# State space layer and feed-forward on one core: the last stage of the kernel tables is placed behind a pair of first weights on VectorE and handed over four steps later

## The chip, the cores and the metric

The kernel runs on one core of a Trainium2 chip. The core has TensorE (PE; PEld is its weight load), VectorE (DVE), ScalarE (ACT), GpSimd (POOL) and SyncE (SP). Here SP, POOL and ACT also start DMA transfers, each through its own queue. The metric is the device time of one execution in microseconds; the profile shows one such execution, instruction by instruction.

## The reference

The input is normalized, and the output is the input plus two branches computed from the normalized tokens `xn` (2048 tokens of 576 channels): a state space layer, applied as a long convolution through Fourier transforms, and a feed-forward block with 4608 hidden units.

```python
def _A_ref(u, A_re, A_im, B_re, B_im, C_re, C_im, log_dt, Dskip):
    dt = jnp.exp(log_dt)[:, None]
    logdA = dt * (A_re + 1j * A_im)
    dB = dt * (B_re + 1j * B_im)
    P = jnp.exp(logdA[:, :, None] * l[None, None, :])
    K = jnp.einsum("dn,dnl,dn->dl", C_re + 1j * C_im, P, dB).real
    ...
def _B_ref(x, w1, w2):
    h = _silu(jnp.einsum("bsd,df->bsf", x, w1))
    return jnp.einsum("bsf,fd->bsd", h, w2)
xn = _layernorm(x, axis=-1)
return x + _A_ref(xn, ...) + _B_ref(xn, B_w1, B_w2)
```

The factor of each of the 576 x 128 states, C·B·dt, is a complex number. The kernel needs it as a magnitude (the table `rhoT`) and a phase in turns (`phiT`). The stage that this change moves is the last part of that phase: it puts the arctangent into the right octant, and the signs with it.

## The kernel before

**Feed-forward on the path of TensorE.** Every float32 operand is split into a high and a low part, and a product is three matmuls (high·high, high·low, low·high). `ffn` goes over two halves of the tokens, over chunks of four tiles of hidden units, and over two blocks of 512 tokens in a half. `up` (line 312 on) makes one hidden tile: 14 matmuls of 512 columns (L320 to L322) into a PSUM tile `ph`, SiLU on ScalarE (`gf`, L328), a copy as the high part `gh` (ScalarE, L329) and the low part `gl` (VectorE, L330). `down` makes an output tile `po` from four hidden tiles: two groups of 12 matmuls of 288 columns (L350), each added to `acc` on VectorE (L355).

**Weights.** `load_w1` brings two tiles of first weights into `w1r`, of which this stretch has a single buffer, with three DMAs on SP's queue (L266 to L268). `split_w1` makes of them the high parts `w1h` (ScalarE, L288) and the low parts `w1l` (VectorE, L290), and remembers the latest low part as `pins["w1l"]`. The next load into the buffer can start once the second low part has been made. Second weights go likewise through `w2r` (SP, L297), a high part (ScalarE, L306) and a low part (VectorE, L308).

**Work beside it.** `side` is a second generator. In it, `phase0` normalizes the later tokens and turns them on TensorE (L125, L130); ScalarE and VectorE take high and low parts out of PSUM (L126, L128, L131, L132; the tile is `xt`), and POOL's queue stores `xt` to DRAM as `dxt` (L241). `natural` makes the tables in stages that are separated by `yield`; the last one is L772 to L782 on VectorE, eleven operations on 96 x 768, with transposes of `br` and `t0` (L689) and copies into `rhoT` and `phiT` (L690). Behind `natural` comes `kgen`, which makes the convolution kernel in 36 chunks: `magic`, `pw` (L806, L808), angles `th` (L838, L840), a rounding pair (ScalarE L854, VectorE L855), absolute value, sine and cosine on ScalarE (L856 to L858), magnitudes `C` and products `S`, `C` on VectorE (L859 to L875). The tiles of `kgen` lie in memory that `phase0` and `natural` have used, so the first of them, `magic`, can be written only when the last store of `xt` has read its tile.

**What sets the order.** `weave` hands the two generators' instructions over in turns: `ffn` has 276 steps, and `side` goes on when its next mark times 276 is reached. A scheduler then orders each engine's instructions, by this order of handing over and by its own idea of when each is ready. `behind(ins)` adds one constraint: what is traced in it stands behind `ins` on that instruction's engine. Each engine, and each DMA queue, takes its instructions in the order so found.

Of the kernel before, what the change touches and what calls it, by code (L numbers as in the profile page):

```python
# [13 lines left out]
ALU = mybir.AluOpType  # L14
# [27 lines left out]
def kernel(  # L42
# [94 lines left out]
    pins = {}  # L137
    wino = {}

    def behind(ins):  # L140
        return tc.issue_after(ins) if ins is not None else nullcontext()

    def spread(up):

        s1 = up.tile([P, 2, P], F32R, name="s1", bufs=1)
        nc.gpsimd.dma_start(s1, cs1)
        for j in range(NJ):
            src = up.tile([P, D], F32, tag="xr", name="xr")
            nc.sync.dma_start(src, dxn[:, j])
            for m in range(2):  # L150
                lo, hi = slice(64 * m, 64 * m + 64), slice(64 - 64 * m, 128 - 64 * m)
                u1 = up.tile([P, D], F32, tag="u1", name="u1")
                sp = up.tile([P, D], F32R, tag="sp", name="sp")
                nc.scalar.copy(sp[lo, :], src[lo, :])
                nc.vector.tensor_sub(sp[hi, :], src[lo, :], sp[lo, :])
                for h in range(2):
                    hs = slice(h * HD, (h + 1) * HD)
                    pu = pss.tile([P, 512], F32, tag="pss", name="pu")
                    nc.tensor.matmul(pu[:, :HD], s1[:, 0, :], sp[:, hs], start=True, stop=False)  # L159
                    nc.tensor.matmul(pu[:, :HD], s1[:, 1, :], sp[:, hs], start=False, stop=True)  # L160
                    nc.scalar.copy(u1[:, hs], pu[:, :HD])  # L161
                nc.gpsimd.dma_start(  # L162
                    d1u.rearrange("(p m j) d -> m j p d", m=2, j=NJ)[m, j], u1)
                yield j
# [46 lines left out]
    def phase0(p0, js):  # L211
        j0 = js[0]
        if j0 < 8:
            xs = load_x(j0, accp, "acc", (nc.sync,))
            acc.update(zip(js, xs))
            yield
        else:
            xs = load_x(j0, p0, "xj", (nc.sync,))
        if j0:
            with behind(pins["xt1"] if j0 == 2 else None):  # L220
                turned(p0, js, norm(p0, js, xs))
        else:
            xn = [norm(p0, (j,), (xj,)) for j, xj in zip(js, xs)]
            last = pins["xn"]
            for j in js:
                turned(p0, (j,), xn[j], None if j else last)
                pins[f"xt{j}s"] = pins["xt_s"]
# [441 lines left out]
    def natural(nat):  # L669
# [3 lines left out]
        v = nc.vector  # L673

        def tl(name):
            return nat.tile([NP, NT, NS], F32, tag=name, name=name)

        def load(ap, name):
            t = tl(name)
            nc.sync.dma_start(t, ap.rearrange("(p t) n -> p t n", t=NT))  # L680
            return t
# [14 lines left out]
        cr, ci = load(c_re, "cr"), load(c_im, "ci")  # L696
# [63 lines left out]
        rc = tl("are")  # L760
# [8 lines left out]
        with behind(last):  # L769
            nc.scalar.mul(t0, t0, 1.0 / (2 * math.pi))  # L770
        yield
        v.tensor_tensor(rc, ci, cr, op=ALU.is_gt)  # L772
        v.tensor_scalar(t1, t0, -2.0, 0.25, op0=ALU.mult, op1=ALU.add)
        v.tensor_mul(t1, t1, rc)
        v.tensor_add(t0, t0, t1)
# [215 lines left out]
    def tail():  # L991

        def last(j):
            y = yp.tile([P, 2, D], F32, tag="yt", name="yt", bufs=2)
            py = [[pool.tile([P, 512], F32, tag=tag, name="py") for pool, tag in pools]
                  for pools in (((ps2, "ps2"), (pss, "pss")), ((pss, "pss"),) * 2)]
            conv((j, j + 1), py)
            for i in range(2):
                for h in range(2):
                    nc.scalar.copy(y[:, i, h * HD:(h + 1) * HD], py[i][h][:, :HD])  # L1000
                conv_load(j + i + AHEAD)
            store(y, j, (nc.gpsimd,), accum_op=ALU.add)

        steps = [(tail_at[0] + j * tail_at[1], conv_load, j) for j in range(AHEAD)]
        steps += [(tail_at[2] + j * tail_at[3], last, j) for j in range(0, 8, 2)]
        for at, f, j in sorted(steps, key=lambda v: v[0]):
            yield at
            with behind(pins["load"]):
                f(j)
# [45 lines left out]
    def gate_of(i):  # L1055

        return (FT + i * 2 * FT + 1) / (2 * NCH * 2 * 2 * FT)

    def side():
        nonlocal s4, kl, yp, pa, kfp, w1x, tail_at  # L1060
        marks = (0.1357, 0.613, 0.855)
        tail_at = (0.893, 0.003, 0.932, 0.005)
        with tc.tile_pool(name="pa", bufs=4) as pa:
            for js in ((0, 1), (2, 3), (4, 5), (6, 7)):
                with behind(pins["xt3"] if js[0] > 2 else None):
                    for _ in phase0(pa, js):
                        if js[0] <= 2:
                            yield 0
                pins[f"xt{js[1]}"], pins[f"xt{js[1]}s"] = pins["xt_v"], pins["xt_s"]
                if js[0] == 2:  # L1070
                    yield 0
            yield 0
        with tc.tile_pool(name="kf", bufs=1) as kfp:
            for n in ("f", "rho", "phi"):
                kf[n] = kfp.tile([P, D], F32, name=n + "T")
            with tc.tile_pool(name="nat", bufs=1) as nat, tc.tile_pool(name="pb", bufs=2) as pb:
                nt = natural(nat)
                tiles = iter(range(8, NJ, 2))
                for at, tables in ((0.0, 1), (0.02, 0), (0.035, 0), (gate_of(1), 1), (0.06, 0), (gate_of(2), 1), (0.08, 0), (0.085, 1)):
                    yield at  # L1080
                    if tables:
                        next(nt, None)
                    else:
                        j = next(tiles)
                        with behind(pins["gl"]):
                            for _ in phase0(pb, (j, j + 1)):
                                pass
            with behind(pins["sd"]):
                nc.gpsimd.dma_start(f1, cf1)
            nc.sync.dma_start(vt, cv)  # L1090
            with tc.tile_pool(name="up", bufs=1) as up, tc.tile_pool(name="w1x", bufs=1) as more:
                sp = spread(up)
                for n, at in enumerate(kgen()):
                    if n > 1:
                        w1x = more
                        next(sp, None)
                    yield marks[0] + at * (marks[1] - marks[0])
                for _ in sp:
                    pass
        w1x = None  # L1100
        s4p = ctx.enter_context(tc.tile_pool(name="s4p", bufs=1))
        s4 = s4p.tile([P, 32], F32, name="s4")
        nc.gpsimd.dma_start(s4, cs4)

        w1x = ctx.enter_context(tc.tile_pool(name="w1y", bufs=1))
        xp = ctx.enter_context(tc.tile_pool(name="xp", bufs=1))
        with tc.tile_pool(name="sx", bufs=1) as sx, tc.tile_pool(name="sy", bufs=1) as sy:
            for k, _ in enumerate(wino_x(sx, sy, xp)):
                yield (171 + k) / 276
        with tc.tile_pool(name="kl", bufs=1) as kl:  # L1110
            for at in spectral():
                yield 176 / 276 + (at - 1) * (marks[2] - 176 / 276)
        yp = ctx.enter_context(tc.tile_pool(name="yp", bufs=3))
        yield from tail()

    sd, fg = side(), ffn()
    for g in (sd, fg, sd, fg, sd, fg, sd):
        next(g)
# [83 lines left out]
```

## Time and profile before

| | |
|---|---|
| median of 3 runs | 1108.33 us (1106.89 to 1108.94) |
| profiled execution | 1107.62 us |
| its span, first to last instruction | 1105.8 us |
| granted TensorE clock | 1.000 |
| instructions in the span | 23079 |

The span lies 1.8 us inside the time of its execution. Times in the views below count from the span's start. A row of the timeline has the start, the duration, engine, line, operation, output <- inputs, shape and count, and in brackets the idle time ahead of it with what ended it. A row of the waits has who waited, for whom, and the total, count and longest in us.

### The profile page before, as it was taken

To read this page: it belongs to the slowest core of one execution; us is meant where nothing else is said; L and a number is where in the kernel's file an instruction comes from. 1 tells how busy PE (TensorE), PEld (TensorE's weight loads), DVE (VectorE), ACT (ScalarE), POOL (GpSimd) and SP (SyncE) were. 2 spreads that over 40 slices of the span, in tenths; PEclk is the share of its full clock that TensorE was granted. 3 is DMA by queue.
4 is the path that set the end of the run, shared out by engine and by line. 5 is a ranking of instruction groups with operands and counts; after the bars stand their busy time and mean duration, and the time that the engine had idled before them with its cause. 6 is when DMAs were issued, how large, how long until landed. Compare 5 with 4: busy or idle time off the path is not lost.

```text
span 1105.8 us, 23079 instructions
## 1 busy us (share of the span) xinstructions
PE 1088.1 (98%) x9101; PEld 985.9 (89%) x9101; DVE 951.8 (86%) x1615; ACT 722.2 (65%) x1283; POOL 143.3 (13%) x249
## 2 busy tenths in 40 slices
PE   6999999999999999999999999999999999999998
PEld 6989899898998888898999989999999999999787
DVE  7699889999999999999999997988888888886323
ACT  4476457677777676767766746888778878775320
POOL 3212100000000000000220001111111221110220
PEclk9999999999999999999999999999999999999999
DMA  9436552355263535457963236465556565554984
GB/s 289 129 128 202 166 165 94 115 148 155 86 170 110 136 131 128 157 116 255 245 208 74 90 82 196 133 183 173 152 162 176 182 176 176 148 161 114 240 220 110
DMA packets 162908, 173.67 MB, mean 157 GB/s; under 512 B 88416, under 2 KB 128624, under 8 KB 162160
## 3 DMA queue, kind: packets, MB, share of 16 engines
q1 hardware_dynamic: 137312, 105.31, 34.3%
q0 software_dynamic: 24320, 65.38, 19.2%
q10 hardware_dynamic: 1168, 1.51, 0.5%
q8 instruction: 72, 1.18, 0.5%
q14 instruction: 36, 0.29, 0.1%
HBM read 109.64 MB, written 62.60 MB: 156 GB/s over the span
## 4 chain that ended last, share of the span: by engine, by line
PE 84%; DVE 7%; DMA 3%; ACT 3%; issue 1%; SPq 1%; POOL 0%; ACTq 0%; POOLq 0%
PE po L350 36%; PE ph L320 17%; PE pb L477 7%; PE pc L477 3%; PE kp L897 3%; PE pk L1031 2%; PE pu L1031 2%; PE pb L1031 2%; PE pa L477 2%; PE z L912 1%; PE ph L322 1%; PE ph L321 1%; PE pc L483 1%; DMA w1r<-in_B_w_dram 1%; PE pu L159 1%
## 5 line engine op out<-in xcount | busy, mean ns | idle before, releaser
L350 PE MATMUL po<-w,gh 128*128 128x288 f32 x2304 | 475.6, 296 | 1.3 <-DVE acc L355 0.9
L350 PEld LDWEIGHTS po<-w,gh 128*128 128x128 f32 x2304 | 375.9, 188 | 17.5 <-issue 3.3
L350 PE MATMUL po<-w,gl 128*128 128x288 f32 x1152 | 333.7, 295 | 0.0
L350 PEld LDWEIGHTS po<-w,gl 128*128 128x128 f32 x1152 | 214.8, 188 | 1.7
L355 DVE TENSOR_TENSOR acc<-po,acc 128x288 f32<-128x288 f32 x296 | 130.3, 452 | 54.3 <-PE po L350 52.9
L320 PE MATMUL ph<-xh,w1h 128*128 128x512 f32 (+1 forms) x368 | 99.7, 388 | 2.4 <-ACT w1h L288 1.1
L320 PE MATMUL ph<-xh,w1l 128*128 128x512 f32 (+1 forms) x368 | 97.8, 382 | 0.1
L320 PE MATMUL ph<-xl,w1h 128*128 128x512 f32 (+1 forms) x368 | 97.7, 383 | 0.0
L328 ACT ACTIVATE gf<-ph 128x512 f32<-128x512 f32 (+1 forms) x92 | 52.9, 578 | 50.5 <-PE ph L322 35.6
L320 PEld LDWEIGHTS ph<-xl,w1h 128*128 128x128 f32 x368 | 67.6, 190 | 13.4
L320 PEld LDWEIGHTS ph<-xh,w1l 128*128 128x128 f32 x368 | 66.2, 188 | 12.2 <-DVE w1l L290 0.3
L320 PEld LDWEIGHTS ph<-xh,w1h 128*128 128x128 f32 x368 | 64.9, 191 | 12.8 <-ACT gf L328 1.5
L162 POOL DMA_DIRECT2D d1u<-u x32 | 17.4, 543 | 402.5 <-ACT u L161 393.5
L854 ACT ACTIVATE c<-th,magic 128x1040 f32<-128x1040 f32 x36 | 42.0, 1168 | 42.0 <-DVE C L875 24.8
L856 ACT ACTIVATE c<-th 128x1040 f32<-128x1040 f32 x36 | 38.6, 1073 | 43.9 <-DVE th L855 43.9
L330 DVE TENSOR_TENSOR gl<-gf,gh 128x512 fp32r<-128x512 f32 (+1 forms) x92 | 60.6, 662 | 4.2 <-ACT gh L329 3.9
L936 POOL DMA_DIRECT2D m<-in_cm_dram x64 | 33.9, 531 | 221.0 <-PE pu L1031 116.4
L329 ACT CAST gh<-gf 128x512 fp32r<-128x512 f32 (+1 forms) x92 | 55.2, 603 | 9.0 <-PE po L350 8.0
L494 DVE TENSOR_TENSOR gl<-gf,gh 128x512 fp32r<-128x512 f32 x56 | 37.8, 688 | 18.2 <-ACT gh L493 17.6
L874 DVE TENSOR_TENSOR S<-th,C 128x1024 f32<-128x1024 f32 x36 | 43.9, 1221 | 7.8 <-ACT th L857 7.6
L838 DVE TENSOR_TENSOR th<-vt,fT 128x1040 f32<-128x1040 f32 x36 | 44.5, 1239 | 0.2
L855 DVE SCALAR_TENSOR_TENSOR th<-c,th 128x1040 f32<-128x1040 f32 x36 | 44.5, 1235 | 0.1
(269 smaller groups left out, 2375.2 us busy)
## 6 DMA issues: line engine op xcount, KB each, us to landing
w1r<-in_B_w_dram SPq DMA_DIRECT2D x35, 512.0 KB, 4.0
dw<-w SPq DMA_DIRECT2D x28, 576.0 KB, 4.7
w<-dw POOLq DMA_DIRECT2D x28, 576.0 KB, 5.7
w2r<-in_B_w_dram SPq DMA_DIRECT2D x44, 288.0 KB, 4.7
d1u<-u POOLq DMA_DIRECT2D x32, 288.0 KB, 2.5
d1k<-stage SPq DMA_DIRECT2D x18, 512.0 KB, 6.1
ul<-d1u SPq DMA_DIRECT2D x32, 288.0 KB, 2.9
kl<-d1k SPq DMA_DIRECT2D x32, 288.0 KB, 3.6
```

The costliest lines, as they stand in the source:

```text
L320: nc.tensor.matmul(ph, w[:, kt, :], v[:, kt, a:e], start=n + kt == 0, stop=False)
L328: nc.scalar.activation(gf, ph, AF.Silu)
L329: pins["gh"] = nc.scalar.copy(gh, gf).ins
L330: pins["gl"] = nc.vector.tensor_sub(gl, gf, gh).ins
L350: pins["pe"] = nc.tensor.matmul(po[:, :HD], gs[g][:, js], ws[:, w, hs], start=n == 0 and j not in begun, stop=n == 3 * len(terms) - 1, ski ...
L355: nc.vector.tensor_add(acc[j][:, hs], po[:, :HD], acc[j][:, hs])
L477: pins["pe"] = nc.tensor.matmul(dst, a[:, kt], v[:, kt], start=start and n == 0, stop=stop and n == 5, skip_group_check=True).ins
L838: nc.vector.tensor_mul(split(th), row(vt[:, 0:65], 65), col(fT, i, 65))
L854: nc.scalar.activation(c65, th, AF.Identity, bias=magic)
L855: nc.vector.scalar_tensor_tensor(th, c65, MAGIC, th, op0=ALU.subtract, op1=ALU.subtract)
L874: nc.vector.tensor_mul(ov3, t[:, :, 0:64].rearrange("n d (x y) -> n d x y", y=32), mv3)
L1031: nc.tensor.matmul(dst, st, mv[:, hs], start=n == 0, stop=n == 3 * len(terms) - 1)
```

## The change

In `natural`, the first operation of the last stage, the comparison at L772, is put behind the latest low part of first weights; the ten operations behind it are handed over as before, and those that read its result follow it. In `side`, the mark of that stage goes from 0.085 to 0.1, so it is handed over at step 28 in place of 24 (0.085 · 276 = 23.5, 0.1 · 276 = 27.6). The same generator then runs on into the first chunk of `kgen`, which is therefore handed over four steps later too.

```diff
         with behind(last):
             nc.scalar.mul(t0, t0, 1.0 / (2 * math.pi))
         yield
-        v.tensor_tensor(rc, ci, cr, op=ALU.is_gt)
+        with behind(pins["w1l"]):
+            v.tensor_tensor(rc, ci, cr, op=ALU.is_gt)
         v.tensor_scalar(t1, t0, -2.0, 0.25, op0=ALU.mult, op1=ALU.add)
...
-                for at, tables in (..., (gate_of(2), 1), (0.08, 0), (0.085, 1)):
+                for at, tables in (..., (gate_of(2), 1), (0.08, 0), (0.1, 1)):
```

The scheduler makes a new order from these two edits. On POOL it is the same as before; on the other engines it differs over the first third of the program and is the same behind that. Lines from 772 on are one higher in the changed file (its L773 is the L772 of before).

The first place is VectorE where the pair of first weights of the third chunk is split (L290); `ci`, `cr` and `t` are the stage's tiles. Before:

```order
L767 TENSOR_TENSOR br<-br,bi 96x768
L772 TENSOR_TENSOR are<-ci,cr 96x768
L355 TENSOR_TENSOR acc_165<-po,acc_165 128x288
L330 TENSOR_TENSOR gl<-gf,gh 128x512
L768 TENSOR_TENSOR br<-br,dh 96x768
L355 TENSOR_TENSOR acc_165<-po,acc_165 128x288
L290 TENSOR_TENSOR w1l<-w1r,w1h 128x640
L774 TENSOR_TENSOR t_921<-t_921,are 96x768
L290 TENSOR_TENSOR w1l<-w1r,w1h 128x640
L330 TENSOR_TENSOR gl<-gf,gh 128x512 x2
```

And now:

```order
L767 TENSOR_TENSOR br<-br,bi 96x768
L355 TENSOR_TENSOR acc_165<-po,acc_165 128x288
L330 TENSOR_TENSOR gl<-gf,gh 128x512
L768 TENSOR_TENSOR br<-br,dh 96x768
L355 TENSOR_TENSOR acc_165<-po,acc_165 128x288
L290 TENSOR_TENSOR w1l<-w1r,w1h 128x640 x2
L773 TENSOR_TENSOR are<-ci,cr 96x768
L330 TENSOR_TENSOR gl<-gf,gh 128x512 x2
```

Two operations of the stage that stood ahead of the second low part stand behind it.

The second place is VectorE at the head of `kgen`; `w_1745` is the fourth tile of second weights of the next chunk. Before:

```order
L308 TENSOR_TENSOR w_1699<-w2r,w_1699 128x576
L330 TENSOR_TENSOR gl<-gf,gh 128x512 x2
L308 TENSOR_TENSOR w_1745<-w2r,w_1745 128x576
L806 MEMSET magic 128x1
L808 MEMSET pw 128x128
L838 TENSOR_TENSOR th<-vt,fT 128x1040 x2
L840 TENSOR_TENSOR th<-th,phiT 128x16x32
L330 TENSOR_TENSOR gl<-gf,gh 128x512
```

And now:

```order
L308 TENSOR_TENSOR w_1699<-w2r,w_1699 128x576
L330 TENSOR_TENSOR gl<-gf,gh 128x512
L807 MEMSET magic 128x1
L809 MEMSET pw 128x128
L839 TENSOR_TENSOR th<-vt,fT 128x1040 x2
L841 TENSOR_TENSOR th<-th,phiT 128x16x32
L330 TENSOR_TENSOR gl<-gf,gh 128x512
L841 TENSOR_TENSOR th<-th,phiT 128x16x32
L308 TENSOR_TENSOR w_1745<-w2r,w_1745 128x576
```

The second `gl` of the pair and the low part of `w_1745` have gone behind `magic` and the first angles. On TensorE the matmuls that read that low part (all of `w_1745`, low and high side by side) have been put later as well, behind two matmuls of the next `up`:

```order
L350 MATMUL po<-w_1699,gl 128x288
L350 MATMUL po<-w_1745,gh 128x288
L320 MATMUL ph<-xh_270,w1h 128x512 x2
L350 MATMUL po<-w_1745,gh 128x288
L350 MATMUL po<-w_1745,gl 128x288
```

The third place is ScalarE at the second chunk of `kgen`. Before:

```order
L854 ACTIVATE c_1928<-th,magic 128x1040
L329 CAST gh<-gf 128x512
L288 CAST w1h<-w1r 128x640 x2
L329 CAST gh<-gf 128x512
L856 ACTIVATE c_1928<-th 128x1040
L328 ACTIVATE gf<-ph 128x512
L857 ACTIVATE th<-th 128x1040
L858 ACTIVATE c_1928<-c_1928,halfpi 128x1040
```

And now:

```order
L855 ACTIVATE c_1928<-th,magic 128x1040
L328 ACTIVATE gf<-ph 128x512
L857 ACTIVATE c_1928<-th 128x1040
L858 ACTIVATE th<-th 128x1040
L859 ACTIVATE c_1928<-c_1928,halfpi 128x1040
L329 CAST gh<-gf 128x512
L288 CAST w1h<-w1r 128x640 x2
L329 CAST gh<-gf 128x512
```

The three activations of the chunk (absolute value, sine, cosine) stand ahead of the casts that TensorE's next `down` and `up` read.

More of the change, by code (lines that the diff above doesn't have):

```diff
@@ L1078, in side @@
                 tiles = iter(range(8, NJ, 2))
-                for at, tables in ((0.0, 1), (0.02, 0), (0.035, 0), (gate_of(1), 1), (0.06, 0), (gate_of(2), 1), (0.08, 0), (0.085, 1)):
+                for at, tables in ((0.0, 1), (0.02, 0), (0.035, 0), (gate_of(1), 1), (0.06, 0), (gate_of(2), 1), (0.08, 0), (0.1, 1)):
                     yield at
```

## The prediction

> **What bounds the kernel now.** I read the page first, then who waits on TensorE, then stretches of 25 us, and the timeline only where the order changes.
>
> ```profile
> PE 1088.1 (98%) x9101; PEld 985.9 (89%) x9101; DVE 951.8 (86%) x1615; ACT 722.2 (65%) x1283; POOL 143.3 (13%) x249
> ```
>
> TensorE is busy for 98% of the span, and no matmul is added or taken away, so the change can move the time only through gaps between matmuls. From 100 to 420 us, the waits of TensorE that the profile shows are these:
>
> ```profile
> PE ph L320 <- ACT w1h L288: 1.1, 1, 1.1
> PE po L350 <- DVE acc L355: 0.9, 1, 0.9
> PE ph L320 <- ACT gf L328: 0.2, 1, 0.2
> ```
>
> There is little to win: 2.2 us in three gaps. Losing is easier, as the stretches show (us; busy and count of PE, PEld, DVE, ACT, POOL; clock, DMA share, GB/s):
>
> ```profile
> 125.00:150.00 25.00, 24.17 (x154) 22.32 (x155) 16.50 (x30) 12.88 (x23) 2.47 (x3) 1.00 0.71 223
> 150.00:175.00 25.00, 25.00 (x146) 22.43 (x145) 24.66 (x41) 13.61 (x18) 0.00 (x0) 1.00 0.19 62
> ```
>
> Until 150 us VectorE has room; from there, with `kgen` on it, it is busy 24.66 of 25 us. Whatever is put behind `kgen`'s first operations waits in a full queue.
>
> **Term 1: the gap at 125 us goes.**
>
> ```profile
> 113.40 0.95 DVE L772 TENSOR_TENSOR are<-ci,cr 96x768 f32<-96x768 f32 x1
> 114.27 0.45 DVE L355 TENSOR_TENSOR acc<-po,acc 128x288 f32<-128x288 f32 x1
> 117.20 0.95 DVE L774 TENSOR_TENSOR t<-t,are 96x768 f32<-96x768 f32 x1
> 118.07 0.81 DVE L290 TENSOR_TENSOR w1l<-w1r,w1h 128x640 fp32r<-128x640 f32 x1
> 118.91 0.39 SPq L266 DMA_DIRECT2D w1r<-in_B_w_dram  x1
> 119.90 0.60 SPq L268 DMA_DIRECT2D w1r<-in_B_w_dram  x1
> DMA to landing us min/median/max: 5.1/5.1/5.1
> 125.06 1.35 ACT L288 CAST w1h<-w1r 128x640 fp32r<-128x640 f32 x2 [2.99 <-DMA w1r<-in_B_w_dram]
> 124.16 0.39 PE L321 MATMUL ph<-x,w1h 128*128 128x512 f32 x1
> 124.38 0.40 PE L322 MATMUL ph<-x,w1l 128*128 128x512 f32 x1
> 125.83 1.19 PE L320 MATMUL ph<-xh,w1h 128*128 128x512 f32 x4 [1.05 <-ACT w1h L288]
> 125.81 0.83 DVE L290 TENSOR_TENSOR w1l<-w1r,w1h 128x640 fp32r<-128x640 f32 x1 [0.74 <-ACT w1h L288]
> ```
>
> The second low part ends at 118.88, and at 118.91 SP starts the next load into the same buffer. Its third piece lands 5.1 us after 119.90 (the landing row is that DMA's own), at 125.0; ScalarE casts at 125.06, and TensorE goes on at 125.83. A matmul of this shape starts 0.22 us after the one ahead (124.16 to 124.38), so 1.45 less 0.22 gives a gap of 1.2 us. The change takes L772 (0.87 to the next start) and L774 (0.87) out from ahead of that low part: the load starts 1.74 us earlier and lands at 123.3, the first cast is through by 124.0 (half of 1.35), and TensorE asks for it at 124.6. **-1.2 us.** It can't be more; it is nothing if the load takes the 1.74 us longer, for which I see no reason.
>
> **Term 2: a low part of second weights gets stuck behind `kgen`'s first wait.**
>
> ```profile
> 142.45 0.69 DVE L330 TENSOR_TENSOR gl<-gf,gh 128x512 fp32r<-128x512 f32 x1 [1.02 <-ACT gh L329]
> 143.64 0.76 DVE L308 TENSOR_TENSOR w<-w2r,w 128x576 fp32r<-128x576 f32 x1 [0.50 <-ACT w L306]
> 147.22 0.06 DVE L806 MEMSET magic<- 128x1 f32 x1 [2.82 <-DMA s<-in_cs_dram]
> 149.72 0.68 DVE L840 TENSOR_TENSOR th<-th,phiT 128x512 f32<-128x512 f32 x1
> 150.33 0.68 DVE L330 TENSOR_TENSOR gl<-gf,gh 128x512 fp32r<-128x512 f32 x1
> 131.32 0.96 POOL L241 DMA_DIRECT2D dxt<-xt  x1 [9.05 <-DVE xt L132]
> 137.72 0.59 ACT L126 CAST xt<-pt 128x512 fp32r<-128x512 f32 x1 [0.33 <-DMA dxt<-xt]
> 138.49 0.68 DVE L128 TENSOR_TENSOR xt<-pt,xt 128x512 fp32r<-128x512 f32 x1
> 139.21 0.28 DVE L132 TENSOR_TENSOR xt<-pt,xt 64x128 fp32r<-64x128 f32 x1
> 139.79 0.96 POOL L241 DMA_DIRECT2D dxt<-xt  x1 [7.51 <-DVE xt L132]
> DMA to landing us min/median/max: 7.2/7.2/7.2
> DMA to landing us min/median/max: 4.1/5.1/8.6
> 148.94 0.29 PE L350 MATMUL po<-w,gl 128*128 128x288 f32 x1
> ```
>
> VectorE idles ahead of `magic` until 147.22. The row names a constant's load, but the tile's memory was `xt`'s, and the store of `xt` begun at 139.79 took 7.2 us: it lands at 147.0. Before, the low part (L308, done at 144.40) and the second `gl` (142.45) stand ahead of this wait; now they stand behind it, and behind two `th` and two L840 besides.
>
> When does the wait end now? The 0.74 us that VectorE idled at 125.81 are gone, so the store begun at 131.32 starts at 130.6 and takes, as before, until L126 at 137.0 (137.72 - 0.74). L128 now stands right behind the `acc` additions, so it starts with L126's end at 137.6, L132 follows 0.72 later and ends at 138.6 (139.49 before): 0.9 us earlier. The store then lands at 146.1, and `magic` starts at 146.3. From `magic` to the first L330 are 3.11 us (147.22 to 150.33); then `gl` 0.60, L840 0.61, L308 0.75: the low part is ready 5.07 us after `magic`, at **151.4**.
>
> When is it wanted? The first matmul to read it is the same number in TensorE's queue as the one that started at 148.94. Two matmuls of 512 columns have come ahead of it for two of 288 (0.22 against 0.14 each, the four at 167.94 in the next fence starting (0.70 - 0.29) / 3 apart; so +0.2), and term 1 brings it 1.2 us forward: 147.9. TensorE waits **3.5 us**, and is 2.3 us later than before.
>
> **Term 3: a high part waits behind three activations.**
>
> ```profile
> 167.27 1.26 DVE L855 SCALAR_TENSOR_TENSOR th<-c,th 128x1040 f32<-128x1040 f32 x1
> 166.58 0.60 ACT L329 CAST gh<-gf 128x512 fp32r<-128x512 f32 x1
> 168.86 1.07 ACT L856 ACTIVATE c<-th 128x1040 f32<-128x1040 f32 x1
> 170.46 1.06 ACT L857 ACTIVATE th<-th 128x1040 f32<-128x1040 f32 x1
> 171.43 1.15 ACT L858 ACTIVATE c<-c,halfpi 128x1040 f32<-128x1040 f32 x1
> 167.94 0.70 PE L350 MATMUL po<-w,gh 128*128 128x288 f32 x4
> 154.97 0.49 DVE L829 TENSOR_TENSOR pw<-pw 128x128 f32<-128x128 f32 x1 [0.21 <-ACT pw L824]
> ```
>
> Before, the cast L329 at 166.58 is done at 167.18, 0.8 us ahead of its matmul at 167.94, while ScalarE waits for L855. Now it stands behind L856 to L858, which can't start before L855 has ended. That end is 168.53, 21.3 us after `magic`; in the new order the stretch between holds one L330 (0.60) and the L308 (0.67, its 0.76 less an overlap like L330's) more and one L355 (0.37 to the next start) less, and I leave out the 0.21 us of idle: 22.0 after `magic`, 168.3. Then 1.07, 1.06, 1.15 and 0.60, less the 0.1 by which they overlap: `gh` at 172.1. TensorE, released at 151.4, would be there at 170.2 (167.94 - 148.94, less the 0.2 already spent): **1.9 us** more of waiting. It now stands 172.1 - 167.94 = **+4.2 us** behind the kernel before. Note that terms 1 and 2 no longer count by themselves: TensorE's place is set by `magic`. On SP's queue the load of `kgen`'s bases (L816) now stands ahead of `xr` and `w1r` and waits for the same memory as `magic`; the casts of that `w1r` stand right behind this `gh`, 26 us after `magic`, against 5.1 us for such a load to land, so I price it at nothing.
>
> **Term 4: what comes after.** In four places, the first behind the L855 of term 3, the new order leaves VectorE little to do between L855 and what needs ScalarE's answer (L874, or an L155 ahead of it): L831, two L833 and at most one L355. The answer takes L856 and L857, 2.1 us. One row shows how often this bites now, the other where TensorE waits for VectorE:
>
> ```profile
> DVE S L874 <- ACT th L857: 7.6, 9, 1.5
> 350.57 0.54 PE L350 MATMUL po<-w,gh 128*128 128x288 f32 x2 [0.88 <-DVE acc L355]
> ```
>
> At up to 1.5 us a place VectorE idles up to 6 us more. Where it comes to 350 us less late than TensorE, the gap there goes (-1.0); where it comes 1.5 us later, TensorE pays that. I take 0, from -1.0 to +1.5.
>
> **Sum.** 1107.62 + 4.2 = 1111.8 us for the profiled execution. The median of the runs is 0.7 above it, which would give 1112.5; I say **1112.0**. The loosest price is the store's landing: 4.1 to 8.6 us in its eight rows, for the 7.2 used, so -3.1 to +1.4. With term 4 that is +0.1 to +7.1; with the median row, 5.1, as the shortest landing and 7.2 as the longest, and term 4 upwards alone, +2.1 to +5.7.
>
> **Rivals.**
>
> (a) *The store lands early.* It has less to share the DMA engines with, since `xr` and `w1r` now come behind it. At the shortest row, 4.1 us, `magic` starts at 143.2; the low part is there at 148.3 and `gh` at 169.0, +1.1 us. About 1109: no change that can be told. Against it: the stores at 131.32 (to L126 at 137.7) and 139.79 took over 6 and 7.2 us, and the second weights' loads and stores of that stretch are still there. 0.17.
>
> The Trainium skill, "DMA: Bandwidth & Descriptors", section "Anatomy of one DMA — SWDGE (gpsimd) path", speaks for this rival: it puts a transfer issued from GpSimd at 2.0 us plus its bytes over 436 GB/s, for 128 x 1152 float32 an estimate of 3.4 us. By that, `magic` would start at 142.5 and the sum would be about +0.4 us. The trace doesn't agree: 7.2 here, and 4.1 at the least.
>
> (b) *Faster: only the gains arrive.* If the low part is there by 147.9, `magic` having started by 142.8, TensorE keeps term 1, and VectorE comes ahead to 350 us, so that the gaps of 1.0 there and 0.2 for L328 go as well: -2.4 us, about 1106. It decides from a landing of 3.7 us downwards, shorter than any of the eight rows. The point moves to longer landings if TensorE comes to that low part later than I count. 0.12.
>
> (c) *VectorE becomes the bound.* At 24.66 of 25 us every us that it idles could reach TensorE by 350 us: 4.2 and 1.5 or more, 1114 to 1116. For it: TensorE waited for VectorE at 350 us already. Against: from 100 us until then it shows no such wait, with VectorE as busy. 0.13.
>
> (d) That the edits change nothing can't be: the new order shows both moves.
>
> **How the numbers follow.** The forecast has 0.58. A difference under 0.2% (2.2 us) is about what can't be told from no change here: 1106.1 to 1110.5. Slower by more are the forecast but for a tenth of it (0.52), (c) (0.13) and of (a) what term 4 pushes over the bound (0.05): 0.70. Faster by more is most of (b), 0.10. The rest, 0.20, is no change. The range goes from the upper end of (b) to the middle of (c): 1107.0 to 1114.8; the forecast's own is 1109.7 (+2.1 on the profiled execution) to 1114.0 (+5.7 on the median).
>
> **What would show it.** Right: no wait at 125 us for L288; VectorE idle ahead of `magic` for longer than 2.82 us; a wait of TensorE in L350 for L308 near 151 us of about 3.5, and one for L329 near 172 us of about 2; the wait at 350 us still there. Wrong: a store from 139 us that lands in under 5 us; or VectorE's idle between L855 and L874 that shows up in TensorE as many small waits from 175 to 350 us; or no wait near 151 us although L308 stands behind `magic`.

## The result, and the profile after

| | kernel before | changed kernel | ratio (95% interval) |
|---|---|---|---|
| time of the runs, median (lowest to highest) | 1107.39 us (1106.42 to 1109.55, 22 runs) | 1109.22 us (1108.16 to 1111.28, 22 runs) | 1.0015 (1.0009 to 1.0022) |
| the profiled execution, and its span | 1107.62, 1105.8 us | 1108.16, 1106.4 us | |

The changed kernel is 1.8 us slower, where 1112.0 was forecast, 3.7 to 4.2 us more. It is less than the 0.2% that the prediction took for what can't be told, but the interval leaves out 1: slower, by little.

The page's first line for the changed kernel (busy time, share of the span and count by engine), and then the waits of TensorE from 100 to 420 us (us in total, times, longest). In the changed file lines from 773 on are one higher, so that L855 of the prediction is L856 here.

```profile
PE 1088.8 (98%) x9101; PEld 986.1 (89%) x9101; DVE 950.3 (86%) x1615; ACT 720.9 (65%) x1283; POOL 143.6 (13%) x249
```

```profile
PE po L350 <- ACT gh L329: 1.4, 1, 1.4
PE po L350 <- DVE acc L355: 1.1, 2, 0.9
PE ph L320 <- ACT gf L328: 0.2, 1, 0.2
PE ph L320 <- ACT w1h L288: 0.2, 1, 0.2
```

The 1.1 us for L288 at 125 us are gone (the 0.2 for L288 here belong to another load, between 200 and 300 us), a wait of 1.4 for the high part L329 is new, and a wait for a low part L308, the forecast's largest term, is not there at all. Now the three places one by one.

**At 125 us** (timeline of the changed kernel: start, length, engine, line; TensorE's rows behind those of the other engines):

```profile
116.03 1.55 DVE L290 TENSOR_TENSOR w1l<-w1r,w1h 128x640 fp32r<-128x640 f32 x2
...
117.49 0.95 DVE L773 TENSOR_TENSOR are<-ci,cr 96x768 f32<-96x768 f32 x1
117.60 0.39 SPq L266 DMA_DIRECT2D w1r<-in_B_w_dram  x1
...
122.15 1.35 ACT L288 CAST w1h<-w1r 128x640 fp32r<-128x640 f32 x2
...
125.32 0.39 PE L322 MATMUL ph<-x,w1l 128*128 128x512 f32 x1
125.54 1.07 PE L320 MATMUL ph<-xh,w1h 128*128 128x512 f32 x4
```

The two low parts stand together, the load starts 1.3 us earlier, the cast is done well ahead, and L320 follows L322 by 0.22 us where it was 1.45.

The load lands 3.3 us earlier, and the earlier start is only 1.3 of that: its third piece (L268) took 3.1 us here, and 5.1 in the profile before. In the eleven other profiles of this document it took 3.1 to 3.4 us. One of the eleven, `store_early` below, has the order of the kernel before up to 135 us, with L772 and L774 still ahead of the low part, and TensorE doesn't wait there (the landing is that of its L268, issued at 121.00):

```profile
DMA to landing us min/median/max: 3.1/3.1/3.1
124.18 1.36 ACT L288 CAST w1h<-w1r 128x640 fp32r<-128x640 f32 x2 [1.03 <-DMA w1r<-in_B_w_dram]
125.69 1.09 PE L320 MATMUL ph<-xh,w1h 128*128 128x512 f32 x4
```

So the gap at 125 us came with one slow landing, and the old order does not have it every time: of two profiles, one. What the change does is to leave room for such a landing: 5.1 us from the new start would end at 123.7, still in time.

**From 135 us to `magic`** (same view; the last row is the landing of the store at 137.81, from the view of that store alone):

```profile
135.88 0.59 ACT L126 CAST xt<-pt 128x512 fp32r<-128x512 f32 x1 [1.74 <-DMA dxt<-xt]
...
137.81 0.96 POOL L241 DMA_DIRECT2D dxt<-xt  x1 [5.90 <-DVE xt L132]
...
138.93 0.33 SPq L310 DMA_DIRECT2D dw<-w  x1
139.30 0.65 SPq L297 DMA_DIRECT2D w2r<-in_B_w_dram  x1
...
142.40 0.06 DVE L807 MEMSET magic<- 128x1 f32 x1 [1.69 <-DMA dxt<-xt]
...
146.68 0.77 DVE L308 TENSOR_TENSOR w<-w2r,w 128x576 fp32r<-128x576 f32 x1
DMA to landing us min/median/max: 4.4/4.4/4.4
```

The store starts at 137.81 and lands in 4.4 us, not 7.2. `magic` comes at 142.4 in place of 147.2, and the low part at 147.45, which is in time. Look at what stands ahead of the store: before, SP's store and load of second weights (138.24 and 138.61) had been issued when it came at 139.79; now they come behind it.

**At 167 us** (same view):

```profile
163.99 1.22 DVE L856 SCALAR_TENSOR_TENSOR th<-c,th 128x1040 f32<-128x1040 f32 x1
...
165.24 1.07 ACT L857 ACTIVATE c<-th 128x1040 f32<-128x1040 f32 x1 [1.77 <-DVE th L856]
...
167.32 1.15 ACT L859 ACTIVATE c<-c,halfpi 128x1040 f32<-128x1040 f32 x1
...
168.38 0.60 ACT L329 CAST gh<-gf 128x512 fp32r<-128x512 f32 x1
...
169.03 0.79 PE L350 MATMUL po<-w,gh 128*128 128x288 f32 x4 [1.37 <-ACT gh L329]
...
352.23 0.53 PE L350 MATMUL po<-w,gh 128*128 128x288 f32 x2 [0.90 <-DVE acc L355]
```

The cast waits for the three activations, and TensorE for the cast. The same matmul started at 167.94 before, so TensorE is here 1.09 us behind. At 350 us the wait for L355 is as before, and TensorE 1.66 us behind (352.23 against 350.57). A part of that is older than the change: at 70 us, before any instruction has moved, this execution was already 0.27 us behind the one before.

### The profile page after: what moved, and what is told of

Same layout as the page of the kernel before. It is cut to its first block, busy times and chain, and to the rows that moved or that the text cites. A ratio compares the mean times of both kernels' runs of the same rounds, so it can differ in the third digit from the quotient of the medians.

```text
span 1106.4 us, 23079 instructions
## 1 busy us (share of the span) xinstructions
PE 1088.8 (98%) x9101; PEld 986.1 (89%) x9101; DVE 950.3 (86%) x1615; ACT 720.9 (65%) x1283; POOL 143.6 (13%) x249
## 4 chain that ended last, share of the span: by engine, by line
PE 78%; DVE 11%; ACT 3%; issue 3%; DMA 2%; SPq 1%; POOL 1%; POOLq 0%; ACTq 0%; DVEq 0%
PE po L350 33%; PE ph L320 15%; PE pb L477 7%; PE pc L477 4%; PE kp L898 3%; PE pk L1032 2%; PE pu L1032 2%; PE pb L1032 2%; PE pa L477 2%; PE z L913 1%; PE ph L322 1%; PE pc L483 1%; PE ph L321 1%; DVE acc L355 1%; DVE C L864 1%
## 5 line engine op out<-in xcount | busy, mean ns | idle before, releaser
L355 DVE TENSOR_TENSOR acc<-po,acc 128x288 f32<-128x288 f32 x296 | 129.7, 450 | 53.8 <-PE po L350 52.6
L320 PE MATMUL ph<-xh,w1h 128*128 128x512 f32 (+1 forms) x368 | 100.3, 389 | 1.6 <-ACT gf L328 0.9
L320 PE MATMUL ph<-xl,w1h 128*128 128x512 f32 (+1 forms) x368 | 98.4, 384 | 0.0
L320 PE MATMUL ph<-xh,w1l 128*128 128x512 f32 (+1 forms) x368 | 98.0, 383 | 0.0
L320 PEld LDWEIGHTS ph<-xl,w1h 128*128 128x128 f32 x368 | 67.9, 191 | 13.2
L320 PEld LDWEIGHTS ph<-xh,w1l 128*128 128x128 f32 x368 | 66.2, 188 | 12.0 <-DVE w1l L290 0.2
L320 PEld LDWEIGHTS ph<-xh,w1h 128*128 128x128 f32 x368 | 64.7, 191 | 12.0 <-ACT gf L328 1.6
L855 ACT ACTIVATE c<-th,magic 128x1040 f32<-128x1040 f32 x36 | 42.0, 1167 | 44.6 <-DVE C L876 28.9
L857 ACT ACTIVATE c<-th 128x1040 f32<-128x1040 f32 x36 | 38.7, 1074 | 47.2 <-DVE th L856 47.1
L329 ACT CAST gh<-gf 128x512 fp32r<-128x512 f32 (+1 forms) x92 | 55.3, 603 | 6.4 <-PE po L350 5.5
L839 DVE TENSOR_TENSOR th<-vt,fT 128x1040 f32<-128x1040 f32 x36 | 44.3, 1234 | 0.2
L856 DVE SCALAR_TENSOR_TENSOR th<-c,th 128x1040 f32<-128x1040 f32 x36 | 44.4, 1232 | 0.1
```

Source lines behind the costliest of these rows:

```text
L320: nc.tensor.matmul(ph, w[:, kt, :], v[:, kt, a:e], start=n + kt == 0, stop=False)
L329: pins["gh"] = nc.scalar.copy(gh, gf).ins
L355: nc.vector.tensor_add(acc[j][:, hs], po[:, :HD], acc[j][:, hs])
L839: nc.vector.tensor_mul(split(th), row(vt[:, 0:65], 65), col(fT, i, 65))
L855: nc.scalar.activation(c65, th, AF.Identity, bias=magic)
L856: nc.vector.scalar_tensor_tensor(th, c65, MAGIC, th, op0=ALU.subtract, op1=ALU.subtract)
```

## The experiments

Neither edit moves an instruction alone. With `behind(pins["w1l"])` and the old mark, and with the new mark alone, every engine's order is the same as before; only both together give the new one. A further `behind` would have the scheduler order the whole program anew. So the runs hold the order of a kernel, engine by engine, with an edge from each instruction to the next (issue order only, no wait is added), and move the few rows that are named. Each diff shows rows of one engine's queue.

**The changed kernel again.** `again` is the changed kernel with its own order so held:

```
for a, b in zip(row, row[1:]):
    tc.add_manual_dep(b, a.name, DependencyInfo(NoSync, DATA))
```

> The changed kernel once more, each engine's order held by edges as the scheduler had found it, as the ground that the other orders stand on. Theory M (the time is set by `magic`, and `magic` by the last store of `xt`): the store starts near 137.8 us, lands in 4 to 5 us, `magic` is near 142.4, the only new wait of TensorE is the one for the high part near 167 us (1.4), and the time is 1.8 us above the kernel before (1.0017). Rival L (the store's landing varies between executions, and the profile showed an early one): this second profile shows a landing of 6 us or more, a wait for the low part near 148 us, and a profiled time 2 us or more above the first one's 1108.16.

Measured: 1108.81 us, ratio 1.0012 (1.0003 to 1.0021). The store landed in 4.4 us again, the new wait is 1.2 us, for the same cast. The early landing was no accident of one profile: it was 4.4 us in all eight profiles in which this store came first. Rival L falls. The profiled execution itself took 1110.16 us, 2 us above the first one, of which 1.0 us was there by 100 us: single executions differ by as much as the change is worth, so that the waits tell more than the totals.

**The store where it was.** `store_late`, on VectorE and in the same way on ScalarE (L126, L131):

```
-L128 TENSOR_TENSOR xt<-pt,xt
-L132 TENSOR_TENSOR xt<-pt_1320,xt
 L330 TENSOR_TENSOR gl<-gf,gh
 L308 TENSOR_TENSOR w_1693<-w2r,w_1693
 L355 TENSOR_TENSOR acc_299<-po,acc_299
+L128 TENSOR_TENSOR xt<-pt,xt
+L132 TENSOR_TENSOR xt<-pt_1320,xt
```

> The order of the changed kernel, but the two parts of the last `xt` tile (L126 and L131 on ScalarE, L128 and L132 on VectorE) stand behind the high and the low part of `w_1693` and one addition, as before the change, so that the store (L241) starts near 139.5 us, behind the first store and load of second weights on SP. Theory M with the landing set by what shares the DMA engines: it lands in 7 us as in the kernel before, `magic` starts at 146.5 to 147, the low part is late by 3 to 4 us at 148 and the high part near 167 by 4 to 4.5 us more, and the time is 4 us above the changed kernel (ratio to the kernel before 1.005 to 1.006): the prediction's 1112 and a little more. With a landing that does not depend on that (4.4 us): `magic` at 144.1, 1.7 us above the changed kernel (1.003). Rival V (`magic` does not set the time): the same as the changed kernel (1.0017).

Measured: 1111.6 us, ratio 1.0035 (1.0021 to 1.0049), 2.8 us above `again`. Its timeline, with the landing of the store at 139.32:

```profile
137.77 0.33 SPq L310 DMA_DIRECT2D dw<-w  x1
138.15 0.43 SPq L297 DMA_DIRECT2D w2r<-in_B_w_dram  x1
...
139.32 0.96 POOL L241 DMA_DIRECT2D dxt<-xt  x1 [7.04 <-DVE xt L132]
...
147.00 0.06 DVE L807 MEMSET magic<- 128x1 f32 x1 [6.45 <-DMA dxt<-xt]
...
151.27 0.75 DVE L308 TENSOR_TENSOR w<-w2r,w 128x576 fp32r<-128x576 f32 x1
...
152.08 0.61 PE L350 MATMUL po<-w,gh 128*128 128x288 f32 x1 [2.74 <-DVE w L308]
DMA to landing us min/median/max: 7.5/7.5/7.5
```

A store that starts 1.5 us later than in the first profile, now behind SP's pair, lands 4.6 us later. The late start alone does not do it: in `store_early` the store starts at 139.92, later still, but ahead of SP's pair, and lands in 4.4 us. All of the forecast's term 2 is here: the low part 5.0 us after `magic`, and a wait of 2.7 us for it.

The time is about the forecast's, in part by luck. At the end of the wait, from 152.0 us on, the granted TensorE clock is 0.50 for 3.4 us, which costs about 1.7 us (an estimate, half of 3.4). That price was in no forecast. In turn the forecast wait of 1.9 us for the cast at 167 us does not come: the cast is done at 172.2 (171.61 + 0.60), as forecast, but TensorE reaches that matmul only at 172.41.

**The low part where it was.** `low_ahead` puts one `gl` and L308 of `w_1745` back ahead of `magic`:

```
+L330 TENSOR_TENSOR gl<-gf,gh
+L308 TENSOR_TENSOR w_1745<-w2r,w_1745
 L807 MEMSET magic
 L809 MEMSET pw
 L839 TENSOR_TENSOR th<-vt,fT x2
 L841 TENSOR_TENSOR th<-th,phiT
-L330 TENSOR_TENSOR gl<-gf,gh
 L841 TENSOR_TENSOR th<-th,phiT
-L308 TENSOR_TENSOR w_1745<-w2r,w_1745
```

> The order of the changed kernel, but the low part of the second weights (L308, `w_1745`) and the `gl` next to it stand ahead of `magic`, as before the change. Theory M: the weights that this low part needs land at 144.8 in the changed kernel, 2.4 us after `magic`, so the low part is made at 145.6 and `magic` starts at 146.3 in place of 142.4; the high part near 167 us comes 3.9 us later, and the time rises by 3.5 to 4 us against the changed kernel, to 5.5 above the kernel before (ratio 1.005). Rival S (the prediction's term 2: the low part behind `magic` is what costs): the time falls by 1 to 2 us against the changed kernel, to the kernel before or 0.5 above it (1.000).

Measured: 1111.85 us, ratio 1.0036 (1.0023 to 1.0048): slower by 3.0 us than `again`. The rows at `magic`, and the wait at the cast:

```profile
145.69 0.67 ACT L306 CAST w<-w2r 128x576 fp32r<-128x576 f32 x1 [2.55 <-DMA w2r<-in_B_w_dram]
...
146.40 0.76 DVE L308 TENSOR_TENSOR w<-w2r,w 128x576 fp32r<-128x576 f32 x1 [2.53 <-ACT w L306]
...
147.10 0.06 DVE L807 MEMSET magic<- 128x1 f32 x1
...
171.79 0.80 PE L350 MATMUL po<-w,gh 128*128 128x288 f32 x4 [2.01 <-ACT gh L329]
```

Since the store now goes first, the weights come later, and a low part that waits for them keeps `magic` waiting. What the forecast took for the loss, the low part behind `magic`, is in this order the better place; rival S falls. `magic` was 3.8 us later than in `again`, and the time rose by 3: theory M's direction, a little less than its size. Not all of it is at the cast: TensorE also waits 0.9 us for an addition (L355) at 155 us.

**The cast where it was, alone.** `cast_ahead` takes L329 of the changed kernel out from behind the activations:

```
+L329 CAST gh<-gf
 L857 ACTIVATE c_1928<-th
 L858 ACTIVATE th<-th
 L859 ACTIVATE c_1928<-c_1928,halfpi
-L329 CAST gh<-gf
 L288 CAST w1h<-w1r x2
```

> The order of the changed kernel, but the high part (L329, `gh_1923`) stands ahead of the three activations of chunk 1 (L857 to L859), as before the change. Theory M (the loss is this cast behind the activations, 26.6 us after `magic`): the wait of 1.4 us near 167 us is gone, the time falls by 1.5 us against the changed kernel, to 0.3 us above the kernel before (ratio 1.0003, from 0.9995 to 1.0010). Rival V (VectorE, which idles for the sine and cosine more often, pays over the whole of the table loop): the time stays at 1.8 us above (1.0017), with the wait moved to a later place.

Measured: 1108.99 us, ratio 1.0014 (1.0005 to 1.0023): nothing won, against theory M. TensorE's wait has only moved to the next row of ScalarE's queue:

```profile
168.75 1.34 ACT L288 CAST w1h<-w1r 128x640 fp32r<-128x640 f32 x2
...
169.52 1.19 PE L320 MATMUL ph<-xh,w1h 128*128 128x512 f32 x4 [1.39 <-ACT w1h L288]
```

**All four casts.** `casts_ahead` puts the two L288 and the next L329 ahead of L857 as well.

> The order of the changed kernel, but all four casts that the change had put behind the activations of chunk 1 (L329 `gh_1923`, two L288 of the first weights, L329 `gh_2062`) stand ahead of L857 to L859, as before the change. With the one cast alone the wait near 167 us only moved to L288, the next in ScalarE's queue, one group of matmuls later. Theory M (what is lost is ScalarE's order there, cast after cast): the wait for L288 is gone as well, TensorE has no wait from 160 to 175 us, and the time falls 1.2 to 1.5 us against the changed kernel, to the kernel before (ratio 0.9995 to 1.0003). Rival V (VectorE cannot wait longer): sine and cosine come 2.4 us later, VectorE idles 2.4 us more ahead of the products, and TensorE waits for an addition (L355) or a `gl` within the next 20 us; the time stays at 1.2 to 1.8 above (1.0011 to 1.0017).

Measured: 1110.71 us, ratio 1.003 (1.002 to 1.0039), by the ratios 1.7 us slower than the changed kernel. VectorE's products and then TensorE:

```profile
169.77 1.23 DVE L875 TENSOR_TENSOR S<-th,C 128x1024 f32<-128x1024 f32 x1 [2.94 <-ACT th L858]
...
171.51 0.45 DVE L355 TENSOR_TENSOR acc<-po,acc 128x288 f32<-128x288 f32 x1
172.02 0.53 PE L350 MATMUL po<-w,gh 128*128 128x288 f32 x2 [1.89 <-DVE acc L355]
...
173.75 0.61 PE L350 MATMUL po<-w,gl 128*128 128x288 f32 x1 [0.81 <-DVE gl L330]
```

The sine comes 2.3 us later, VectorE stands idle for it 2.94 us, and in its queue the addition and the `gl` that TensorE needs stand behind those products. Theory M's claim that it is ScalarE's order alone falls; it was rival V that named the addition, but the time lies above its range too. One reason shows in this profile: from 173.4 us on, within the second wait, the granted TensorE clock is 0.50 for 3.4 us.

**The same on both engines.** `supply_ahead` has the four casts ahead and, on VectorE:

```
+L330 TENSOR_TENSOR gl<-gf,gh
+L355 TENSOR_TENSOR acc_165<-po,acc_165
+L290 TENSOR_TENSOR w1l<-w1r,w1h x2
+L330 TENSOR_TENSOR gl<-gf,gh
 L875 TENSOR_TENSOR S<-th,C
 L876 SCALAR_TENSOR_TENSOR S<-th,C
-L355 TENSOR_TENSOR acc_165<-po,acc_165
```

> The changed kernel with what TensorE is fed by near 170 us ahead of chunk 1's sine and products on both engines, as before the change: on ScalarE the four casts ahead of L857 to L859, on VectorE one addition (L355), two `gl` (L330) and two low parts of first weights (L290) ahead of L875. With the casts alone TensorE waited 2.1 us for that addition, which stood behind the products. Theory Q (the loss is where chunk 1's chain stands in the two queues together, whichever engine one looks at): no wait from 160 to 180 us, TensorE keeps the 1.3 us of 125 us, less the 0.5 us it lost at 113 us, and the time is 1.5 us under the changed kernel: ratio to the kernel before 0.9988 to 1.0002. Rival V (the table loop cannot be later): sine, cosine and products come 4 us later than in the changed kernel, the next rounding pair and so the loop with them, and TensorE pays before 300 us: 1.001 or more.

Measured: 1108.05 us against 1107.17 before, ratio 1.0003 (0.9994 to 1.0012; the medians alone would give 1.0008). No wait is left from 160 to 175 us. TensorE's waits from 100 to 420 us:

```profile
PE po L350 <- DVE acc L355: 1.2, 2, 0.9
PE kp L898 <- issue: 0.3, 1, 0.3
PE ph L320 <- DVE w1l L290: 0.3, 1, 0.3
PE ph L320 <- ACT gf L328: 0.2, 1, 0.2
```

That is just above theory Q's range, and rival V's 1.001 is still inside the interval. The profile says how much of each is true. At 170 us TensorE is 1.7 us earlier against the changed kernel than at 165 us, as Q has it. But 0.9 us of that are lost again before 250 us, as V has it: 0.4 at 176 us (the 0.3 for L898, a matmul that reads `kgen`'s products) and 0.5 at 246 us (the 0.3 for L290). Undone on both engines, the order gives back the loss at its place and keeps about half of what it gave; undone on ScalarE alone, it gives back nothing or costs more. VectorE alone was not tried.

**Term 1 alone.** `gain_alone` and `gain_again` are one kernel: the one before, with

```
-L772 TENSOR_TENSOR are<-ci,cr
 L355 TENSOR_TENSOR acc_165<-po,acc_165
 L330 TENSOR_TENSOR gl<-gf,gh
 L768 TENSOR_TENSOR br<-br,dh
 L355 TENSOR_TENSOR acc_165<-po,acc_165
-L290 TENSOR_TENSOR w1l<-w1r,w1h
-L774 TENSOR_TENSOR t_921<-t_921,are
-L290 TENSOR_TENSOR w1l<-w1r,w1h
+L290 TENSOR_TENSOR w1l<-w1r,w1h x2
+L772 TENSOR_TENSOR are<-ci,cr
+L774 TENSOR_TENSOR t_921<-t_921,are
```

> The kernel before, with one move: the two operations of the table stage that stood ahead of the second low part (L772 and L774) stand right behind it. Term 1 by itself: the wait of 1.1 us for L288 at 125 us is gone, nothing else moves on the other engines, and the time is 1.2 us under the kernel before (ratio 0.9989, from 0.9980 to 0.9998). Rival N (a microsecond won at 125 us is lost again where the next wait ends, at `magic` or at 350 us): 1.0000, with a longer wait there.

> The kernel before with L772 and L774 behind the second low part, once more. In the first profile TensorE was 1.34 us earlier against the kernel before from 125 us to the end, but the timed runs gave 0.9997 (0.9988 to 1.0005). If the 1.3 us are real in timed runs, the ratio is 0.9988 (0.9980 to 0.9997); if another stretch takes them back, 1.0000.

Measured: 1107.2 us (ratio 0.9997, 0.9988 to 1.0005) and 1106.8 us (0.9997, 0.9989 to 1.0006). In both profiles the wait at 125 us is gone: TensorE's lead on the kernel before, matmul by matmul, improves by 1.3 us there. In the first profile it keeps most of that to the end; in the second it loses 0.9 us of it at 167 us. Here is why, first from `gain_alone`:

```profile
146.82 0.06 DVE L806 MEMSET magic<- 128x1 f32 x1 [3.40 <-DMA dxt<-xt]
...
166.47 0.48 DVE L355 TENSOR_TENSOR acc<-po,acc 128x288 f32<-128x288 f32 x1
```

and the same from `gain_again`, with the wait that follows:

```profile
148.17 0.06 DVE L806 MEMSET magic<- 128x1 f32 x1 [4.73 <-DMA dxt<-xt]
...
167.49 0.44 DVE L355 TENSOR_TENSOR acc<-po,acc 128x288 f32<-128x288 f32 x1
167.99 0.53 PE L350 MATMUL po<-w,gh 128*128 128x288 f32 x2 [0.81 <-DVE acc L355]
```

The store took 1.4 us longer (8.2 against 6.8), `magic` and VectorE's addition came 1.35 and 1.02 us later, and TensorE, which was earlier by then, waited for that addition. So a part of the gain is lost again in some executions. In others there is nothing to gain, as the old order without the gap in `store_early` shows. The timed runs show 0.4 us, which can't be told from none; how much of the missing 0.9 either cause takes stays open.

**The store early in the kernel before.** `store_early` moves L126, L131, L128 and L132 ahead as the change does, and leaves the rest.

> The kernel before, with the two parts of the last `xt` tile (L126 and L131 on ScalarE, L128 and L132 on VectorE) ahead of the high and the low part of `w_1693`, as the change has it. If the store's landing is set by whether the first store and load of second weights of that stretch are ahead of it, it starts near 138.5 us, ahead of SP's pair, and lands in 4.4 us instead of 7.2. If the landing is the transfer's own (7 us) it lands at 145.5. In both cases the low part of `w_1745` stands ahead of `magic`, which cannot start before it; TensorE waited for nothing that hangs on `magic` here, so the time is that of the kernel before (0.9995 to 1.0005).

Measured: 1111.23 us, ratio 1.003 (1.002 to 1.0039). The landing came out as the first theory said, 4.4 us, and the time as nobody had: 3.6 us more. The rows of the wait, and one of those behind it:

```profile
149.01 0.67 ACT L306 CAST w<-w2r 128x576 fp32r<-128x576 f32 x1 [5.78 <-DMA w2r<-in_B_w_dram]
...
149.73 0.74 PE L350 MATMUL po<-w,gh 128*128 128x288 f32 x2 [3.00 <-ACT w L306]
150.51 0.68 PE L350 MATMUL po<-w,gh 128*128 128x288 f32 x2
```

SP's load, issued at 141.42 in this run, took 7.6 us behind the store, against 4.3 ahead of it in the kernel before. The high part of `w_1745` came 3 us too late, and TensorE lost 4.8 us there, not 3: from 149.9 us on the granted clock is 0.50 for 3.4 us, and matmuls of 288 columns start 0.24 us apart instead of 0.13. What the store gains, the load behind it pays; the changed kernel gets by, since its store and its load are issued 2.1 us earlier than here (137.81 and 139.30, against 139.92 and 141.42), and its load lands at 144.8.

**One more wait taken out.** `both_fixed` is `casts_ahead` with the first of the two additions at 350 us moved ahead of L839 and L831 on VectorE.

> The changed kernel with the four casts ahead of L857 to L859, and one more move on VectorE: at 350 us the first of two additions (L355), for which TensorE waits 0.9 us in both kernels, stands ahead of the angles (L839) and the squares (L831) instead of behind them. Theory M: term 1's gain stays, the casts' loss is gone, and the wait at 350 us is gone too: 1.2 us under the kernel before or a little more (0.9980 to 0.9992). Rival V: whatever VectorE saves TensorE at 350 us it takes back at the next addition or product; the time is that of the run with the four casts alone.

Measured: 1110.99 us, ratio 1.0029 (1.0018 to 1.004), the same as `casts_ahead`. The wait at 350 us is gone, and 40 us on stands a longer one, which had been 0.2 in the kernels before and after:

```profile
393.99 1.19 PE L320 MATMUL ph<-xh,w1h 128*128 128x512 f32 x4 [1.21 <-ACT gf L328]
```

The 1.0 us is taken back there in full, as rival V said.

No version beats the kernel before by more than its interval; `gain_alone` comes nearest.

## Why the prediction was wrong in size

**Term 1 (-1.2) is right against the one profile that it was read from, and not for the kernel.** Between L322 and L320 at 125 us TensorE won 1.45 - 0.22 = 1.23 us. But the term took the landing of 5.1 us for a fixed one, and it was 3.1 to 3.4 in every other profile; with the 3.1 us of `store_early` the old order has no gap there. That its number came out is luck: the one profile of before has the slow landing, and the gain is measured against it. In timed runs the two moves of term 1 are worth 0.4 us, which can't be told from none.

**Term 2 (a wait of 3.5) is the step that failed, at its first number.** The prediction said "the store then lands at 146.1, and `magic` starts at 146.3", from the 7.2 us that the landing took before. It took 4.4, and `magic` started at 142.4. What follows in the term held: from `magic` to the low part 5.05 us, where 5.07 was worked out. `store_late`, with a landing of 7.5, has the low part at 152.0 (forecast 151.4) and a wait of 2.7 (forecast 3.5).

Two things were missed. The store before that one, begun at 130.73, was taken to last "as before" until 137.0, and L126 came at 135.88. And the order on VectorE had changed at this very place: L128 and L132 stood now ahead of L308 of `w_1693`, on which SP's store and load hang. The prediction used this to start the store 0.9 us earlier, and not to ask which transfer then comes first. Its argument against rival (a), that "the second weights' loads and stores of that stretch are still there", was true, but they were there behind the store.

**So rival (a) came true,** the store that lands early, nearly number for number: it worked out `gh` at 169.0, TensorE 1.1 us behind and about 1109 us; measured are 168.98, 1.09 and 1109.2. It had 0.17. That the numbers meet so closely is partly luck: `magic` came 0.8 us earlier than (a) had it, and the end of L856 0.8 us later behind `magic`. Nor was it for the reason that (a) gave, `xr` and `w1r` coming later: in `store_late` they come even later, at 147.63 and 148.27, and the store still takes 7.5 us. Rival (b), which needed a landing of 3.7 us or less, did not come. The Trainium skill, "DMA: Bandwidth & Descriptors", section "Anatomy of one DMA — SWDGE (gpsimd) path", gave an estimate of 3.4 us for this transfer; the 4.4 measured is nearer to that than to 7.2.

**Term 3 was right in its mechanism.** L856 ended 22.8 us after `magic` (22.0 worked out), and the cast behind the three activations made TensorE wait 1.4 us. The 1.9 worked out were for a TensorE held up by term 2; where that came, in `store_late`, this wait was nothing, since TensorE came there 2.2 us later than worked out (172.41 against 170.2), some 1.7 of it by the half clock. The prediction had no price for that clock. It priced the casts L288 behind it at nothing; that holds only as long as TensorE already waits for the cast ahead of them. `cast_ahead`, `casts_ahead` and `supply_ahead` show that the price belongs to chunk 1's place in both queues, not to the one cast.

**Term 4 (0) was right, within its range.** VectorE's idle time ahead of the products, which had been 7.6 us over nine places, rose to this:

```profile
DVE S L875 <- ACT th L858: 10.3, 11, 1.5
```

TensorE felt little of it: the wait at 350 us stayed at 0.9, and from 173 to 349 us it fell behind by another 0.4. So rival (c), VectorE as the bound with 1114 to 1116, did not come; that it has no room to give is what `casts_ahead` and `both_fixed` show.

**What stays open.** A wait of 0.2 us for L355 near 114 us was not foreseen, and TensorE is 0.5 us later there than at 112 us; it isn't traced further. Waits won and lost add up to about 1.3 us from 112 to 385 us in the profiles (0.40 behind at the one, 1.67 at the other); the timed medians say 1.8 and 1.2. That fits, but is no proof that nothing else costs a few tenths. The 1.3 us have the gap at 125 us in them; against an execution of the kernel before without that gap the loss would be about 2.6 us (an estimate, 1.27 and the 1.3 won there). How many executions have the gap isn't known. Nor is it shown what made the one landing slow.

## What to carry to other kernels

A landing time read from a trace holds for the transfers around it, and for that execution. Before it is used for a changed order, look which transfers of the other queues start within a few us of it on either side, and whether the change swaps them: here 1 to 2 us at the start were worth 3 us at the landing. A gap that hangs on one landing is looked for in a second profile of the same order before a gain is booked for closing it: here 5.1 us became 3.1, and the gap was gone. And where a chain runs to and fro between two engines' queues, look at both before one order is undone: on ScalarE alone, the wait moved here to the next row, or to the other engine.

## What the runs showed of the hardware

**Transfers of two queues lengthen each other.** Of the three transfers below, on POOL's and SP's queues, those issued first were done first, and the later ones paid. The store (576 KB) and the first pair of second weights on SP (a store of 576 KB and a load of 288 KB), issue to landing:

| run | first issued | store of `xt` | SP's store | SP's load |
|---|---|---|---|---|
| changed kernel | store of `xt` | 4.4 us | 5.2 us | 5.5 us |
| `again` | store of `xt` | 4.4 us | 5.4 us | 5.8 us |
| `low_ahead` | store of `xt` | 4.4 us | 5.5 us | 5.9 us |
| `store_early` | store of `xt` | 4.4 us | 5.8 us | 7.6 us |
| kernel before | SP's pair | 7.2 us | 3.1 us | 4.3 us |
| `store_late` | SP's pair | 7.5 us | 3.1 us | 3.6 us |
| `gain_alone` | SP's pair | 6.8 us | 3.1 us | 3.6 us |
| `gain_again` | SP's pair | 8.2 us | 3.1 us | 3.6 us |

The store that goes first takes the same time in every run, 4.4 us the one and 3.1 the other; the store of `xt` that goes second varies by over a microsecond between executions of one kernel (6.8 and 8.2). This is no rule of first come, first served: in the lower four runs SP's next store, also of 576 KB, was issued 0.5 us behind the store of `xt` and landed 0.5 to 1.8 us before it.

**A wait of TensorE can cost more than its length.** The granted clock went to 0.50 for 3.4 us at the end of waits of 3.00 us (`store_early`) and 2.74 us (`store_late`), and in the second of two waits close together, 1.89 and 0.81 us, in `casts_ahead`. The same two waits in `both_fixed`, and the 2.01 us in `low_ahead`, left the clock at 1.00. At half clock 3.4 us are worth about 1.7 (an estimate), and at the wait of 3.00 us TensorE lost 4.8.
